# Input products of five FFN groups by a 2x2x2 Strassen scheme in an HGRN2 + maxout-FFN kernel

## The chip, the cores and the metric

The kernel runs on one core of one Trainium2 chip, in one launch. The metric is the device time in microseconds of that core. Times are given for the whole execution; the profile's span, which most views refer to, is a little shorter.

## What is computed

A recurrent attention block (4 batches, 8 heads, 768 steps, head size 48) feeds a feed-forward block with three input projections and a maximum over them, all in float32:

```python
for t in range(S):
    state = f[:, :, t, :, None] * state + np.einsum('bhd,bhe->bhde', k[:, :, t], v[:, :, t])
    y[:, :, t] = np.einsum('bhd,bhde->bhe', q[:, :, t], state)      # f = sigmoid(f_logit)
...
h = np.maximum(np.maximum(x @ w1, x @ w2), x @ w3)                  # x: (3072, 384), w: (384, 768)
return (h @ w_out).astype(np.float32)                               # w_out: (768, 384)
```

The weights come as 64-bit floats and are rounded to 32 bits in the kernel.

## The kernel before, in words

**Units and groups.** Attention is done in 24 units `u`, each 64 steps of two batches (128 tokens), in order. Four units make a group of TOK = 512 tokens; there are six groups, numbered 0 to 5 in the code and 1 to 6 in this text. The attended tokens of a group are kept transposed in `xT`, 128 partitions by NK = 3 blocks of 128 features by 512 tokens. When a group's attention is complete, its feed-forward part is queued as a generator in `pending`, and runs beside the attention of the next group.

**Attention of a unit.** ScalarE makes the gates (`sigmoids`, L296 or L299). VectorE scans the decays (L317, L335), transposes blocks of 32 (L284; L370 for `ks`, sixteen a unit), masks the score matrix (`at`, L383) and updates the state (L432). GpSimd multiplies the decays into keys and queries (`kh` L328, `qh` L339) and into the state (L345). TensorE forms scores (`pairs`, L380), values and state sums (`values`, L399 and L424) and the state's part (`finish`, L470). `finish` then copies the result to `heads` on ScalarE (L476), and `pack` (L484) moves it into `xT` by ten small DMAs on SP's queue: slots 0 to 2 of a group together, slot 3 alone, the latter at units 8, 12, 16, 20 and after unit 23. At the very end the ten are split between SP and ScalarE.

**Feed-forward of a group.** In groups 2 to 6 the maximum is taken relative to w1: `apart` (L545) has replaced w2 and w3 by their differences from w1, and `linear` (L561) has replaced w1 by w1 times w_out, so that the output is x times that (L528) plus the maximum of 0, x(w2-w1) and x(w3-w1), times w_out (L532). `ffn` (L605) makes, for each of six column blocks j, two products of three 128x128x512 matmuls (`product`, L511); ScalarE takes the first with Relu into `top` (L612), VectorE the maximum with the second into `hm` (L614). Then `outputs` (L524) makes four blocks of 128 tokens, each three matmuls L528 and six L532 of 384 columns, a ScalarE copy (L537) and two stores on SP. Products and outputs use the two PSUM buffers of pool `ps_f`; the two of `ps_tr` serve transposes, which units from 8 on no longer need. Group 1 (`ffn_first`, L572) does all three products, rounds the weights as they arrive, and does `apart`, the transposes of w1 (`turn`, L552) and `linear` behind its products.

**Order of the work.** The order on each engine is the order in which the code is written (`manual_schedule`). The main loop (L728) goes unit by unit, and between the steps of attention calls `fill`, which takes pieces of queued feed-forward work until their cost, 4/2.4 ns a column (COLUMN), has used up a budget. Each unit grants five times PART = 2740 ns (L643). An unused budget is kept while nothing is queued:

```python
def fill(ns):
    budget[0] += ns
    while budget[0] > 0 and pending:
        try:
            budget[0] -= next(pending[0])
        except StopIteration:
            pending.pop(0)
```

**Weights.** `load_weights` (L201) brings 24 pieces as 64-bit words into RAW = 12 staging buffers `raw`; `round_begin` and `round_end` turn them into float32 with `top_bits` (four buffers) and `rest_bits` (three). From unit 11 on `check_range` (L261) reads the pieces again on ScalarE and looks for values out of range, with the same buffers.

Of the kernel before, what the change touches and what calls it, by code (L numbers as in the profile page):

```python
# [9 lines left out]
FP32 = mybir.dt.float32  # L10
I32 = mybir.dt.int32
U32 = mybir.dt.uint32
AF = mybir.ActivationFunctionType
# [42 lines left out]
def kernel(  # L56
# [33 lines left out]
    def fast():  # L90
        ctx = ExitStack()
        with ctx:
# [100 lines left out]
            pieces = [(w_in[i][:, :, j * 128:(j + 1) * 128], src[:, j * 128:(j + 1) * 128])  # L193
                      for j in range(NJ) for i, src in enumerate((moe_w1, moe_w2, moe_w3))]
            pieces += [(w_out[:, j:j + 1, :], moe_w_out[j * 128:(j + 1) * 128, :]) for j in range(NJ)]
            RAW = 12
            PIECE = NK * 128
            raw, raw_next = {}, []

            def load_weights(count, done=0, queue=nc.sync):  # L200

                for n in range(len(raw_next), min(len(raw_next) + count, done + RAW, len(pieces))):
                    raw_next.append(n)
                    dst, src = pieces[n]
                    a = dst.shape[1]
                    if src.dtype != FP32:
                        raw[n] = work.tile([128, 2 * PIECE], U32, name="raw", bufs=RAW)
                        dst, src = raw[n].rearrange("p (a c) -> p a c", a=a), src.bitcast(U32)
                    queue.dma_start(out=dst, in_=src.rearrange("(a p) c -> p a c", a=a))

# [9 lines left out]

            BY_VECTOR = 9

            def round_begin(n):
                if n in raw:
                    lo, hi = words(n)
                    top = work.tile([128, PIECE], U32, name="top_bits", bufs=4)
                    if n >= BY_VECTOR:

                        nc.scalar.activation(top.bitcast(FP32), hi.bitcast(FP32), AF.Sign)
                        nc.scalar.mul(top.bitcast(FP32), top.bitcast(FP32), -2.0)  # L230

                    rest = work.tile([128, PIECE], U32, name="rest_bits", bufs=3)
                    nc.scalar.activation(rest, lo, AF.Copy, scale=2.0 ** -29)
                    halfway[n] = (top, rest)

# [17 lines left out]
            def check_load(n):  # L253
                src = pieces[n][1]
                if src.dtype != FP32:
                    raw[n] = work.tile([128, 2 * PIECE], U32, name="raw", bufs=RAW)
                    a = pieces[n][0].shape[1]
                    nc.sync.dma_start(out=raw[n].rearrange("p (a c) -> p a c", a=a),
                                      in_=src.bitcast(U32).rearrange("(a p) c -> p a c", a=a))

            def check_range(n):  # L261

                if n in raw:
                    _, hi = words(n)
                    size = work.tile([128, PIECE], FP32, name="top_bits", bufs=4)
                    over = work.tile([128, PIECE], FP32, name="rest_bits", bufs=3)
                    nc.scalar.activation(size, hi.bitcast(FP32), AF.Abs)
                    nc.scalar.activation(over, size, AF.Relu, scale=-1 / HI_MIN, bias=1.0,
                                         accum_out=outside[:, 2 * n:2 * n + 1])
                    nc.scalar.activation(over, size, AF.Relu, bias=-HI_END * (1 - 2.0 ** -24),  # L270
                                         accum_out=outside[:, 2 * n + 1:2 * n + 2])
                    raw.pop(n)
# [245 lines left out]
            def new_hm():  # L518
                return work.tile([128, NJ, TOK], FP32, name="hm", bufs=1)

            def new_top(w):
                return work.tile([128, TOK], FP32, name="top")[:, 0:w]
# [38 lines left out]
            def linear(a):  # L561

                p = ps_f.tile([128, TOK], FP32, name="p")
                for j in range(NJ):
                    nc.tensor.matmul(p[:, 0:DM], lhsT=w_in[0][:, a, j * 128:(j + 1) * 128], rhs=w_out[:, j, :],  # L565
                                     start=(j == 0), stop=(j == NJ - 1))
                    if j % 2:
                        if j == NJ - 1:
                            nc.scalar.copy(w_lin[:, a, :], p[:, 0:DM])
                        yield 2 * DM * COLUMN  # L570

            def ffn_first(xT):  # L572
                hm = new_hm()
# [22 lines left out]
                for i in range(GRP):  # L596
# [2 lines left out]
                    yield from outputs(0, hm, i)  # L599
                    for j in range(i * NJ // GRP, (i + 1) * NJ // GRP):  # L600
                        yield from turn(j)
                for a in range(NK):
                    yield from linear(a)

            def ffn(g, xT):  # L605
                hm = new_hm()
                for j in range(NJ):
                    for i in (1, 2):
                        p = yield from product(g, xT, j, i, slice(0, TOK))
                        if i == 1:  # L610
                            top = new_top(TOK)
                            nc.scalar.activation(top, p, AF.Relu)  # L612
                        else:
                            nc.vector.tensor_tensor(hm[:, j, :], p, top, op=ALU.max)  # L614
                        yield TOK * COLUMN
                for i in range(GRP):
                    yield from outputs(g, hm, i, xT)

# [425 lines left out]
```

## Time and profile before

| | |
|---|---|
| device time, median of 3 runs | 458.1 us (457.14 to 458.23) |
| the profiled execution | 457.98 us |
| its span | 456.2 us |
| granted TensorE clock | 1.00 |
| L511, 128x512, 432 records | 195.3 us busy |
| L532 and L528, 128x384, 408 records | 99.3 and 42.4 us busy |
| L370, 224 transposes of 32 rows | 67.7 us busy, 302 ns each |
| L614, 30 maxima of 512 columns | 681 ns each |
| L612, 30 Relu of 512 columns | 594 ns each |
| L328 and L339 on GpSimd, 512 columns | 1960 and 1176 ns each |
| `xT<-heads` DMAs | 588 ns between issues, 2.0 us from issue to landing (medians) |

The profile is of one execution. "Busy" is the time in which an engine has an instruction in work; "PE" are matmuls, "PEld" the loads of their stationary operand, DVE VectorE, ACT ScalarE, POOL GpSimd, SPq the queue of SyncE. A float32 matmul leaves two records. The columns of a group of instructions are: line, engine and operation, output<-inputs, shape and number, then busy time and the mean of one, then the engine's idle time ahead of them with what ended it. In a timeline the first number is the start from the begin of the span, the second the length, both in microseconds.

### The profile page before, as it was taken

The page shows a single profiled execution, that of the slowest core. Times are in us where ns is not written, and L with a number is a line of the kernel's source. Part 1 is how long each engine was busy: PE and PEld are TensorE (multiplying, and loading weights), DVE is VectorE, ACT ScalarE, POOL GpSimd, SP SyncE. Part 2 cuts the span into 40 slices and gives each one's busy share as a digit, 9 for nine tenths or more (in the row PEclk, how much of TensorE's full clock was granted, in tenths as well). Part 3 has the DMA queues.
Part 4 walks back from the last instruction along what each step waited for, and adds up shares of the span by engine and source line. Part 5 has one row for each costly group of instructions (what it writes and reads, how often), then busy time and mean ns, then how long its engine had stood idle before and what let it go on. Part 6 is the DMA issues. An engine that isn't in the chain of part 4 may idle for free.

```text
span 456.2 us, 10209 instructions
## 1 busy us (share of the span) xinstructions
PE 432.9 (95%) x4062; PEld 244.1 (54%) x4062; DVE 253.4 (56%) x510; ACT 150.1 (33%) x350; POOL 103.9 (23%) x125
## 2 busy tenths in 40 slices
PE   4989999999999999999999999999989999999995
PEld 3777655556554456554456654455544455544553
DVE  6976757556858569357779557759456520011100
ACT  2434757403312214414414524504324331111000
POOL 2153654403033033032033023023032120000000
PEclk9999999999999999999999999999999999999999
DMA  8889997202547733647763557643746003100011
GB/s 169 213 245 299 259 205 89 36 19 71 94 66 88 133 93 72 147 78 146 92 164 77 147 104 131 98 142 72 165 78 124 2 0 88 45 9 0 4 35 37
DMA packets 177140, 47.13 MB, mean 103 GB/s; under 512 B 154816, under 2 KB 175552, under 8 KB 177088
## 3 DMA queue, kind: packets, MB, share of 16 engines
q1 hardware_dynamic: 173616, 45.64, 47.6%
q10 hardware_dynamic: 3472, 0.79, 0.8%
q8 instruction: 33, 0.54, 0.5%
q14 instruction: 19, 0.16, 0.1%
HBM read 37.75 MB, written 4.72 MB: 93 GB/s over the span
## 4 chain that ended last, share of the span: by engine, by line
PE 84%; DVE 5%; ACT 4%; DMA 4%; issue 2%; SPq 1%; POOL 0%; ACTq 0%; DVEq 0%
PE p L511 42%; PE p L532 18%; PE p L528 7%; PE y L470 3%; PE p L565 3%; PE y L399 2%; PE y L424 2%; PE a L380 2%; DVE r L317 2%; DMA raw<-in_moe_w_out_dram 2%; ACT heads L476 1%; PE tr L279 1%; DMA xT<-heads 1%; ACT sig L299 1%; PE y L395 1%
## 5 line engine op out<-in xcount | busy, mean ns | idle before, releaser
L511 PE MATMUL p<-xT,w_in 128*128 128x512 f32 (+1 forms) x504 | 212.8, 569 | 7.5 <-ACT top L612 2.8
L511 PEld LDWEIGHTS p<-xT,w_in 128*128 128x128 f32 x504 | 92.0, 190 | 104.2 <-issue 85.2
L532 PE MATMUL p<-w_out,hm 128*128 128x384 f32 x288 | 99.3, 491 | 1.3 <-ACT w_in L558 1.0
L532 PEld LDWEIGHTS p<-w_out,hm 128*128 128x128 f32 x288 | 53.6, 190 | 37.1 <-ACT w_in L558 1.3
L370 DVE STREAM_TRANSPOSE ks<-kh 32x128 f32<-32x128 f32 x224 | 67.7, 302 | 3.5
L614 DVE TENSOR_TENSOR hm<-p,top 128x512 f32<-128x512 f32 x30 | 20.4, 681 | 80.9 <-PE p L511 80.5
L327 POOL COPY ends<-r 128x8 f32<-128x8 f32 x24 | 6.7, 279 | 187.0 <-DVE r L317 187.0
L612 ACT ACTIVATE top<-p 128x512 f32<-128x512 f32 x30 | 17.8, 594 | 91.9 <-PE p L511 91.9
L383 DVE TENSOR_TENSOR at<-a,mask 128x512 f32<-128x512 f32 x24 | 16.6, 692 | 48.8 <-PE a L380 48.8
L528 PE MATMUL p<-w_in,xT 128*128 128x384 f32 x120 | 42.4, 489 | 0.0
L537 ACT COPY o<-p 128x384 f32<-128x384 f32 x24 | 11.4, 477 | 93.6 <-PE p L532 90.1
L476 ACT COPY heads<-y 64x256 f32<-64x256 f32 (+1 forms) x60 | 22.1, 369 | 54.9 <-PE y L470 45.5
L328 POOL TENSOR_TENSOR kh<-kt,r 128x512 f32<-128x512 f32 x16 | 31.4, 1960 | 35.4 <-DVE kt L284 33.2
L317 DVE TENSOR_TENSOR_SCAN r<-gate,from_one 128x520 f32<-128x520 f32 x24 | 29.8, 1241 | 6.6 <-ACT gate L296 3.4
L528 PEld LDWEIGHTS p<-w_in,xT 128*128 128x128 f32 x120 | 22.5, 190 | 16.0 <-issue 1.9
L335 DVE TENSOR_TENSOR_SCAN prod<-gate,from_inv 128x520 f32<-128x520 f32 x24 | 30.2, 1257 | 0.0
L247 POOL TENSOR_TENSOR w_in<-top_bits,rest_bits 128x384 uint32<-128x384 uint32 x18 | 20.8, 1161 | 26.6 <-DVE top_bits L241 12.1
L339 POOL TENSOR_TENSOR qh<-qt,prod 128x512 f32<-128x512 f32 x16 | 18.8, 1176 | 6.2 <-DVE qt L284 6.2
L345 POOL TENSOR_TENSOR state<-st,ends 128x384 f32<-128x384 f32 x22 | 18.9, 857 | 0.2
L399 PEld LDWEIGHTS y<-at,v_ld 64*64 64x64 f32 x640 | 11.2, 134 | 13.0 <-issue 6.1
L380 PE MATMUL a<-qh,kh 48*64 48x64 f32 x768 | 15.7, 219 | 1.0 <-DVE qh L339 0.8
L470 PEld LDWEIGHTS y<-qh,state 48*48 48x48 f32 x640 | 10.3, 119 | 11.7 <-issue 11.7
(101 smaller groups left out, 366.3 us busy)
## 6 DMA issues: line engine op xcount, KB each, us to landing
raw<-in_moe_w_dram SPq DMA_DIRECT2D x36, 384.0 KB, 5.5
v_ld<-in_v_dram SPq DMA_DIRECT2D x48, 96.0 KB, 3.1
raw<-in_moe_w_out_dram SPq DMA_DIRECT2D x12, 384.0 KB, 4.9
out_dram<-o SPq DMA_DIRECT2D x47, 96.0 KB, 2.2
xT<-heads SPq DMA_DIRECT2D x30, 72.0 KB, 2.2
f_ld<-in_f_logit_dram SPq DMA_DIRECT2D x32, 64.0 KB, 2.7
k_ld<-in_k_dram SPq DMA_DIRECT2D x32, 64.0 KB, 2.7
q_ld<-in_q_dram SPq DMA_DIRECT2D x32, 64.0 KB, 2.9
```

The source lines that it names most:

```text
L247: nc.gpsimd.tensor_tensor(dst, by(top), by(rest), op=ALU.add)
L317: nc.vector.tensor_tensor_scan(r[:, 0:LEN][:, ::-1], flat(gate)[:, ::-1], flat(from_one)[:, ::-1], 1.0, op0=ALU.mult, op1=ALU.max)
L328: (nc.vector if u < BY_ROWS else nc.gpsimd).tensor_tensor(kh.rearrange("p h a t -> p a h t"), kt, by_batch(r[:, 1:LEN + 1].rearrange("p (x ...
L335: nc.vector.tensor_tensor_scan(flat(prod), flat(gate_tiles[u % 2]), flat(from_inv[u % 2]), 1.0, op0=ALU.mult, op1=ALU.max)
L370: nc.vector.transpose(ks[n * 32:(n + 1) * 32, :, par, e0:e0 + 32], kh[p0:p0 + 32, :, a, t0:t0 + 32])
L380: nc.tensor.matmul(p[t, par, hp * C:(hp + 1) * C], lhsT=kh[r, hp, a, :], rhs=qh[r, a, hp, :], start=True, stop=True)
L470: nc.tensor.matmul(y[o:o + D, a, hp * C:(hp + 1) * C], lhsT=st[r, a, hp, :], rhs=d["qh"][r, a, hp, :], start=False, stop=(hp == HP - 1), s ...
L476: nc.scalar.copy(heads[o, :, t0 + a * C:t0 + (a + 1) * C], y[i, a, 0:HP * C].rearrange("p (h t) -> p h t", h=HP))
L511: nc.tensor.matmul(p if g or w < TOK else p.rearrange("p (two t) -> p two t", two=2), lhsT=w_in[i][:, kt, j * 128:(j + 1) * 128], rhs=rhs, ...
L528: nc.tensor.matmul(p[:, 0:DM], lhsT=xT[:, kt, i * UT:(i + 1) * UT], rhs=w_lin[:, kt, :], start=(kt == 0), stop=False)
L532: nc.tensor.matmul(p[:, 0:DM], lhsT=hm[:, j, i * UT:(i + 1) * UT], rhs=w_out[:, j, :], start=(g == 0 and j == 0), stop=(j == NJ - 1))
L614: nc.vector.tensor_tensor(hm[:, j, :], p, top, op=ALU.max)
```

## The change

For groups 2 to 6 the input products are rearranged. The 512 tokens are split into two halves of 256, the two weight differences are taken together with two of the three feature blocks, and that 2x2x2 product is done with seven multiplications in place of eight; the third feature block is multiplied as before. Two column blocks share a PSUM bank. In this way a pair of column blocks takes 22 matmuls of 256 columns. Sums of tokens (`sx`, four of 128x256 a group) are made by VectorE; sums of weights (`mixed`) are made once, by five subtractions of 128x768 between the steps of `linear`, which is cut in halves. The results of the seven banks are joined by ScalarE (two copies, one Relu a pair), VectorE (five sums or maxima, one scalar_tensor_tensor) and GpSimd (two sums). Banks come in turn from `ps_f` and `ps_tr`. To make room, weights are staged in nine buffers, four of which (`raw_kept`) later hold the mixed weights, and the temporaries are shared with `top_bits` and `rest_bits`, now 512 columns wide. PART and the main loop stay.

```diff
-            RAW = 12
+            RAW, RAW_KEPT = 9, 4
+
+            def new_raw(kept=False):
+                return work.tile([128, 2 * PIECE], U32, name="raw_kept" if kept else "raw",
+                                 bufs=RAW_KEPT if kept else RAW - RAW_KEPT)
...
-                        raw[n] = work.tile([128, 2 * PIECE], U32, name="raw", bufs=RAW)
+                        raw[n] = new_raw(n % RAW >= RAW - RAW_KEPT)
...
+            def new_temp(name):
+                return work.tile([128, TOK], FP32, name=name, bufs=4 if name == "top_bits" else 3)
...
-                for a in range(NK):
-                    yield from linear(a)
+                for n in range(NJ):
+                    if n < 5:
+                        mix(n)
+                    yield from linear(n // 2, n % 2)
+
+            mixed = {}
+            first, second = w_in[1], w_in[2]
+
+            def mix(n):
+
+                if n == 0:
+                    mixed.update({i: new_raw(True).bitcast(FP32) for i in (2, 3, 4, 5)})
+                    mixed[1] = second[:, 0]
+                out, x, y = ((mixed[3], second[:, 1], second[:, 0]), (mixed[1], second[:, 0], first[:, 0]),
+                             (mixed[2], second[:, 1], mixed[1]), (mixed[4], first[:, 1], mixed[2]),
+                             (mixed[5], first[:, 2], second[:, 2]))[n]
+                nc.vector.tensor_tensor(out, x, y, op=ALU.subtract)
 
             def ffn(g, xT):
+
                 hm = new_hm()
-                for j in range(NJ):
-                    for i in (1, 2):
-                        p = yield from product(g, xT, j, i, slice(0, TOK))
-                        if i == 1:
-                            top = new_top(TOK)
-                            nc.scalar.activation(top, p, AF.Relu)
-                        else:
-                            nc.vector.tensor_tensor(hm[:, j, :], p, top, op=ALU.max)
-                        yield TOK * COLUMN
+                X = lambda k, half: xT[:, k, half * HALF:(half + 1) * HALF]
+                sx = work.tile([128, 4, HALF], FP32, name="sx", bufs=1)
+                S = lambda n: sx[:, n - 1]
+                two = lambda t: t.rearrange("p (j t) -> p j t", j=2)
+                turn_of = [0]
+
+                def bank(j, *terms):
+                    turn_of[0] += 1
+                    p = ps_f.tile([128, TOK], FP32, name="p") if turn_of[0] % 2 else ps_tr.tile([128, TOK], FP32, name="tr")
+                    for jj in range(2):
+                        for n, (w, x) in enumerate(terms):
+                            nc.tensor.matmul(p[:, jj * HALF:(jj + 1) * HALF], lhsT=w[:, (j + jj) * 128:(j + jj + 1) * 128],
+                                             rhs=x, start=(n == 0), stop=(n == len(terms) - 1))
+                    return p, 2 * len(terms) * HALF * COLUMN
+
+                def add(out, x, y, op=ALU.add, engine=nc.vector):
+                    engine.tensor_tensor(out, x, y, op=op)
+
+                for j in range(0, NJ, 2):
+                    out = [hm[:, j:j + 2, h * HALF:(h + 1) * HALF] for h in range(2)]
+                    p, cost = bank(j, (first[:, 0], X(0, 0)))
+                    e1 = new_temp("top_bits")
+                    nc.scalar.copy(e1, p)
+                    yield cost
+                    p, cost = bank(j, (first[:, 1], X(1, 0)), (first[:, 2], X(2, 0)))
+                    a = new_top(TOK)
+                    add(a, p, e1)
+                    yield cost
+                    if j == 0:
+                        add(S(3), X(0, 0), X(0, 1), ALU.subtract)
+                        add(S(1), X(0, 1), X(1, 1))
+                        add(S(2), S(1), X(0, 0), ALU.subtract)
+                        add(S(4), X(1, 0), S(2), ALU.subtract)
+                    p4, cost = bank(j, (mixed[4], X(1, 1)), (mixed[5], X(2, 1)))
+                    yield cost
+                    p, cost = bank(j, (mixed[1], S(1)))
+                    e5 = new_temp("top_bits")
+                    nc.scalar.copy(e5, p)
+                    d = new_temp("rest_bits")
+                    add(d, p4, e5, ALU.max)
+                    yield cost
+                    p, cost = bank(j, (mixed[2], S(2)))
+                    m = new_temp("top_bits")
+                    add(m, p, e1)
+                    add(d, d, m, engine=nc.gpsimd)
+                    yield cost
+                    p, cost = bank(j, (second[:, 1], S(4)), (second[:, 2], X(2, 0)))
+                    q = new_temp("rest_bits")
+                    add(q, p, e5)
+                    add(q, q, m, engine=nc.gpsimd)
+                    yield cost
+                    p, cost = bank(j, (mixed[3], S(3)), (second[:, 2], X(2, 1)))
+                    add(out[1], two(p), two(d))
+                    nc.scalar.activation(out[1], out[1], AF.Relu)
+                    nc.vector.scalar_tensor_tensor(out[0], two(a), 0.0, two(q), op0=ALU.max, op1=ALU.max)
+                    yield cost
                 for i in range(GRP):
                     yield from outputs(g, hm, i, xT)
```

The seven banks of a pair are called bank 1 to bank 7 in this text, in the order of the code. In the changed kernel the products stand at L644, `at` at L390, `ks` at L377, L424 at L431, L470 at L477, L528 at L535, L532 at L539, and the DMAs of `pack` at L498.

More of the change, by code (lines that the diff above doesn't have):

```diff
@@ L225, in round_begin @@
                     lo, hi = words(n)
-                    top = work.tile([128, PIECE], U32, name="top_bits", bufs=4)
+                    top = new_temp("top_bits")[:, 0:PIECE].bitcast(U32)
                     if n >= BY_VECTOR:
@@ L230, in round_begin @@
                         nc.scalar.mul(top.bitcast(FP32), top.bitcast(FP32), -2.0)
-                    rest = work.tile([128, PIECE], U32, name="rest_bits", bufs=3)
+                    rest = new_temp("rest_bits")[:, 0:PIECE].bitcast(U32)
                     nc.scalar.activation(rest, lo, AF.Copy, scale=2.0 ** -29)
@@ L255, in check_load @@
                 if src.dtype != FP32:
-                    raw[n] = work.tile([128, 2 * PIECE], U32, name="raw", bufs=RAW)
+                    raw[n] = new_raw()
                     a = pieces[n][0].shape[1]
@@ L264, in check_range @@
                     _, hi = words(n)
-                    size = work.tile([128, PIECE], FP32, name="top_bits", bufs=4)
-                    over = work.tile([128, PIECE], FP32, name="rest_bits", bufs=3)
+                    size = new_temp("top_bits")[:, 0:PIECE]
+                    over = new_temp("rest_bits")[:, 0:PIECE]
                     nc.scalar.activation(size, hi.bitcast(FP32), AF.Abs)
@@ L559, in turn, with linear @@
                 yield DM * COLUMN
-            def linear(a):
-                p = ps_f.tile([128, TOK], FP32, name="p")
-                for j in range(NJ):
-                    nc.tensor.matmul(p[:, 0:DM], lhsT=w_in[0][:, a, j * 128:(j + 1) * 128], rhs=w_out[:, j, :],
+            lin = {}
+            def linear(a, half):
+                if half == 0:
+                    lin[a] = ps_f.tile([128, TOK], FP32, name="p")
+                p = lin[a][:, 0:DM]
+                for j in range(half * NJ // 2, (half + 1) * NJ // 2):
+                    nc.tensor.matmul(p, lhsT=w_in[0][:, a, j * 128:(j + 1) * 128], rhs=w_out[:, j, :],
                                      start=(j == 0), stop=(j == NJ - 1))
[L567 to L570, printed above, removed]
+                if half:
+                    nc.scalar.copy(w_lin[:, a, :], p)
+                yield NJ // 2 * DM * COLUMN
             def ffn_first(xT):
@@ L605, in ffn @@
             def ffn(g, xT):
                 hm = new_hm()
-                for j in range(NJ):
-                    for i in (1, 2):
-                        p = yield from product(g, xT, j, i, slice(0, TOK))
-                        if i == 1:
-                            top = new_top(TOK)
-                            nc.scalar.activation(top, p, AF.Relu)
-                        else:
-                            nc.vector.tensor_tensor(hm[:, j, :], p, top, op=ALU.max)
-                        yield TOK * COLUMN
+                X = lambda k, half: xT[:, k, half * HALF:(half + 1) * HALF]
```

## Prediction

> **What bounds the kernel now.** I read the page's busy shares first, then the groups by shape, the stretches from one group of tokens to the next, and the timeline at the seams between groups.
>
> ```profile
> PE 432.9 (95%) x4062; PEld 244.1 (54%) x4062; DVE 253.4 (56%) x510; ACT 150.1 (33%) x350; POOL 103.9 (23%) x125
> ...
> L511 PE MATMUL p<-xT,w_in 128*128 128x512 f32 x432 | 195.3, 600 | 6.6 <-ACT top L612 2.8 <-DVE hm L614 1.9 <-DMA xT<-heads 1.8
> L614 DVE TENSOR_TENSOR hm<-p,top 128x512 f32<-128x512 f32 x30 | 20.4, 681 | 80.9 <-PE p L511 80.5
> ```
>
> TensorE is busy nearly always; VectorE waits for it (80.5 us before L614), hardly ever the reverse (1.9 us). So work taken from TensorE shortens the span, as long as nothing else is late. Now the stretches between the ends of L470 at group seams (each line: the stretch, its length, then the busy time of PE, PEld, DVE, ACT and POOL):
>
> ```profile
> 119.60:187.80 68.20, 66.84 (x644) 35.63 (x635) 46.22 (x103) 16.18 (x37) 16.31 (x16) 1.00 0.52 94
> 187.80:254.90 67.10, 65.55 (x685) 35.20 (x688) 46.01 (x102) 25.64 (x66) 16.36 (x16) 1.00 0.59 118
> 254.90:323.80 68.90, 67.33 (x680) 35.88 (x672) 46.07 (x102) 25.87 (x67) 16.33 (x16) 1.00 0.57 114
> 323.80:390.70 66.90, 64.34 (x608) 33.58 (x599) 27.30 (x50) 22.10 (x58) 12.27 (x12) 1.00 0.33 70
> 390.70:451.40 60.70, 60.59 (x174) 30.75 (x166) 4.97 (x11) 6.66 (x15) 0.00 (x0) 1.00 0.09 21
> ```
>
> TensorE fills every stretch, the last (no attention left) without a gap, but in three of them VectorE already has 46 us of 67 to do. Last, the timeline (start, length): a run of 256-column products, the seam at 323 and the seam at 390.
>
> ```profile
> 42.65 2.76 PE L511 MATMUL p<-xT,w_in 128*128 128x256 f32 x12
> 45.24 0.60 PE L279 MATMUL tr<-ident,q_ld 128*128 128x128 f32 x4
> ...
> 323.36 0.66 PE L470 MATMUL y<-qh,state 48*48 48x64 f32 x32
> 326.77 6.79 SPq L491 DMA_DIRECT2D xT<-heads  x10
> 331.50 1.12 PE L511 MATMUL p<-xT,w_in 128*128 128x512 f32 x2
> 334.47 1.96 PE L511 MATMUL p<-xT,w_in 128*128 128x512 f32 x4 [1.84 <-DMA xT<-heads]
> ...
> 390.73 2.20 PE L528 MATMUL p<-w_in,xT 128*128 128x384 f32 x6
> 391.95 3.59 SPq L491 DMA_DIRECT2D xT<-heads  x5
> 392.77 4.03 PE L532 MATMUL p<-w_out,hm 128*128 128x384 f32 x12
> 396.64 23.34 PE L511 MATMUL p<-xT,w_in 128*128 128x512 f32 x54
> 419.91 0.19 PE L792 MATMUL tr<-is_feature,least 128*1 128x1 f32 x2
> ```
>
> A matmul is two records. The reader is to see that at a seam the last quarter of xT travels by ten DMAs, which land some 10 us after L470 (6 us at the last seam, where two queues share the issues), and that outputs of the group before (L528, L532) fill just that time.
>
> [...] here a float32 load takes 190 ns (L511 PEld)[...] four transposes take 0.86 us from 6.85 to 7.71, and 0.44 us from 18.00 to 18.44. [...] L383 has 692. [...] L339 takes 1176 ns and the same size at L328 1960 ns[...].
>
> **The change, part by part.** The sum is made against the profiled execution, 457.98 us (span 456.2), beside a median of 458.1.
>
> *Matmuls.* A group had 36 products of 512 columns (6 column blocks, 2 weights, 3 feature blocks); now 3 pairs of blocks with 11 terms, 2 blocks each, are 66 products of 256 columns. 512 columns: from 396.64 to 419.91 are 27 matmuls, 0.862 us each, up to 0.87 in the run behind it; I take 0.864. 256 columns: 42.65 to 45.24 are 6 in 2.59 us, 0.432 each. Five groups: 180 x 0.864 = 155.5 us become 330 x 0.432 = 142.6: **-12.9 us**. Two weight loads (2 x 0.19 = 0.38) still fit under 0.432, but barely; bounds -8 (0.447 a product) and -14.
>
> *Seams.* fill() counts columns. A group costs its budget 51.2 us (28.2 + 23.0) instead of 53.8, while PART, five times for each of four units, still grants 54.8. So outputs are used up earlier, and in the order of the changed program less of them stands behind the last L470 of a group. Bank 3 of the new scheme is the first to read the second half of xT; in front of it stand banks 1 and 2, 6 x 0.432 = 2.6 us, and one product of its own.
> Seam at unit 12: L380 0.6, three blocks of three outputs 5.8, L399 and L424 1.2 and banks 2.6 make 10.2 us against a landing after 9.5: nothing. At 8: over 14 us: nothing.
> At 16: 0.6 + 1.9 + 1.2 + 3.0 = 6.7 us, landing after 9.3 (first issue 256.14, last 262.4, 1.9 to land; L470 ends at 255.0): +2.5.
> At 20: L380 and the banks alone, 3.6 us, landing after 10.4 (334.4 less 324.0), or 9 if SP is free at once: about +6.2, where now 1.8 are lost: +4.4.
> Last seam: 3.0 us against 5.9 (390.7 to 396.6): +2.9, since the 5.9 us of L528 and L532 that covered it are now done before.
> Behind the waiting bank 3 stands all of TensorE's later work. The half-width sums wait for the same DMAs on VectorE; behind them stand kt, the scan prod and qt, and GpSimd waits for these, but it is TensorE that ends last there.
> Sum **+9.8**, bounds 3 and 13.
>
> *VectorE.* Removed for each group: 6 maxima, 4.1 us. Added: 15 of 512 columns with PSUM, 0.65 from start to start, 3 scalar_tensor_tensor of two SBUF inputs (no row; 0.65 to 1.1 from L550, 650 ns for 384; I take 0.7) and 4 sums of half width (0.42, from L585): 13.5 us. A unit of attention costs it 16 x 0.302 (L370) + 3 x 0.70 (L284) + 1.24 + 1.26 + 0.21 + 0.69 + 0.53 = 10.9. In the product stage, some two units long, that is 21.8 + 13.5 = 35.3 us, against 28.5 + 2 x 2.3 = 33.1 of TensorE. VectorE works in order: what is late behind its new operations is the mask of `at`, the transposes of ks (L424 waits) and the release of banks. Following the order through group 3 (unit 12) by hand: bank 4 waits 1.1 for the half-width sums, L424 0.7 for ks, the first output 1.1 for hm, whose last step waits for GpSimd (kh 1.96, qh 1.18, state 0.83, then two new additions of 1.2 to 2.0): 2.9 us, where 1.5 are lost now (0.7 + 0.6 + 0.2). Group 2 comes to 2.1 for 1.3. Four groups: 0.8 + 1.4 + 1.4 + 0.8, the last with half the ks work: about **+4**, bounds 0 and 11. Four banks instead of two is why it isn't more. In group 6 VectorE is free, nothing is added.
>
> *ScalarE*: nine operations of 0.59 for six, +1.8 us a group, under 26 of 67 busy: nothing. Its new Relu waits for VectorE's sum into hm, and behind it queue the copy of the next pair's first bank and the heads copies; four banks bear that wait. *GpSimd*: 30 additions, 6 a group; only the wait above.
>
> *Start*: five subtractions of 768 columns (1.0 to 1.3 us each from L550), spread between VectorE's work while 18 products L565 run; nine instead of twelve staged weight pieces still lead their use by six roundings. **+0.5**, bounds 0 and 3: SP would hold loads queued behind a piece whose buffer GpSimd has not freed.
>
> *Clock*: of the 6 us at unit 20 about 4.5 lie in one piece[...]. Half a chance: **+1**, bounds 0 and 3.5.
>
> Sum: -12.9 + 9.8 + 4 + 0.5 + 1 = +2.4, so **460.4 us**.
>
> **Rivals.** (1) *The seams stay covered, not slower.* Place: bank 3 at units 16, 20 and the end; price: up to 9.8 us; it decides below about 6 us in all. For it: SP may issue earlier where the outputs' stores are already gone, and a TensorE delayed by VectorE gives the DMAs time. Against it: heads copies, ten issues of 0.65 and 1.9 to land are fixed. With 3.5 us at the seams, 3 at VectorE and 0.5 at the start: -5.9, 452 us. (2) *VectorE becomes the bound.* For it: 35 of 33 us[...]; against it: four banks, and output stages in which it can catch up. +10 instead of +4: 466.5. (3) *The narrow products don't keep 0.432 us*, since loads leave 0.05 of it: at 0.447, 465.
>
> **How the numbers follow.** Forecast 0.45 (own range 457 to 463.5), rival 1 0.28, rival 2 0.18, rival 3 0.09. The range 451.5 to 467 leaves out the lower end of rival 1 and the upper of 2. A measurement of this kernel tells about 0.3%, 1.4 us, from no change: below 456.6 lies most of rival 1, 0.27; between, its rest and the lower part of the forecast, 0.18; above 459.4, 0.55.
>
> **What would show it.** (Lines of the changed kernel here: L644 the products, L431 today's L424.) L644 x660 records near 0.216 us from start to start; PE's waits of L644 for DMA xT<-heads of 2 to 7 us near units 16, 20 and the end; VectorE busy near 300 us, 56 of 66 in a group's stretch; L644 and L431 (ks) waiting for DVE, 2 to 3 us a group. Wrong if the seams show no gap of TensorE over 2 us, or if its gaps inside the product stages sum to over 15 us.

## The result, and the profile after

| | before | changed |
|---|---|---|
| device time, median | 457.6 us (456.18 to 458.23, 4 runs) | 474.9 us (473.24 to 475.2, 4 runs) |
| the profiled execution | 457.98 us | 474.79 us |
| its span | 456.2 us | 473.1 us |
| mean granted TensorE clock | 1.00 | 0.977 |

The ratio is 1.0375 (95% interval 1.0339 to 1.0411): 17 us slower. The forecast was 460.4 us with a range up to 467; the sign was right, the size was not.

First the page of the changed kernel: busy times, and the clock that was granted in 40 slices of the span.

```profile
PE 433.1 (92%) x4362; PEld 308.8 (65%) x4362; DVE 306.9 (65%) x595; ACT 157.7 (33%) x365; POOL 144.0 (30%) x155
...
PEclk9989999999999999999999989989979999999999
```

TensorE was busy for 432.9 us before and is for 433.1 now, although its products need 12.9 us less. "Busy" counts a matmul at half clock at nearly twice its length (six records of L644 take 2.90 us in place of 1.53, below), so the saving must have been eaten inside the busy time as well as in gaps. The clock row says where: slices below 9 near 30, 278, 313 and 349 us (a slice is 11.8 us long; the half clock from 294.46 to 297.88 us lies across a border, and hides in two 9s). In the profile of before no slice lies below 9. Next, what TensorE waited for (in total, times, longest):

```profile
PE p L644 <- DMA xT<-heads: 13.9, 7, 6.7
PE tr L644 <- DVE rest_bits L649: 4.7, 2, 2.4
PE y L431 <- DVE ks L377: 3.7, 8, 1.3
PE p L644 <- DVE rest_bits L649: 2.0, 1, 2.0
```

For xT it was 1.8 us before. The stretches between the starts of L477 at the seams (stretch, length, busy time of PE, PEld, DVE, ACT and POOL, clock, DMA share, GB/s), to be set beside those of before in the prediction:

```profile
121.24:191.08 69.84, 66.80 (x730) 48.69 (x729) 61.52 (x126) 17.75 (x40) 25.64 (x22) 1.00 0.48 86
191.08:262.98 71.90, 67.44 (x729) 48.38 (x729) 55.58 (x118) 27.78 (x70) 23.83 (x22) 1.00 0.58 115
262.98:340.33 77.35, 70.32 (x724) 51.07 (x723) 56.00 (x118) 27.14 (x69) 23.90 (x22) 0.93 0.51 103
340.33:412.38 72.05, 64.06 (x654) 46.73 (x653) 36.64 (x66) 23.44 (x60) 20.40 (x18) 0.95 0.31 67
412.38:473.00 60.62, 53.41 (x241) 39.09 (x240) 14.13 (x27) 8.68 (x17) 7.60 (x6) 0.99 0.09 21
```

The second to fourth were 67 to 69 us and are now 72, 77 and 72; VectorE has gone from 46 to 56 us in two of them. The clock stands below 1 in the two that grew most. Last, the seam that the prediction showed at 323 us, now at 340:

```profile
340.33 0.66 PE L477 MATMUL y<-qh,state 48*48 48x64 f32 x32
...
342.36 1.89 PE L644 MATMUL tr<-xT,w_in 128*128 128x256 f32 x8
...
350.91 1.19 PE L644 MATMUL p<-xT,raw_kept 128*128 128x256 f32 x2 [6.66 <-DMA xT<-heads]
352.83 2.90 PE L644 MATMUL p<-xT,raw_kept 128*128 128x256 f32 x6 [0.73 <-DMA xT<-heads]
355.52 1.22 PE L644 MATMUL tr<-sx,w_in 128*128 128x256 f32 x4
356.57 1.03 PE L644 MATMUL p<-sx,raw_kept 128*128 128x256 f32 x4
```

Two banks cover 2.6 us, then nothing is ready for 6.7 us. And then look at the lengths: six records of bank 3 take 2.90 us where six take 1.53 at the last seam (at 419.01, with the clock at 1.00). It is the same instruction; the clock that was granted from 349.07 to 355.90 us is 0.50.

**The sum.** Taking TensorE's records from start to start, the 16.8 us between the two profiled executions split as follows: products -12.9; gaps and waits at the seams +12.1 (13.9 less 1.84); VectorE's lateness +7.4 (4.7 us more of gaps on L649, L377 and the like, and 2.7 inside the records of L431, 13.28 to 15.97); half clock +8.9, an estimate: half of the 17.8 us in which TensorE was busy at a granted clock of 0.50 (six windows of 3.41 us, so up to 1.7 us for each); the rest, shared among transposes and the start, +1.3.

### The profile page after: what moved, and what is told of

It is laid out like the page before. It is cut to its first block, busy times and chain, and to the rows that moved or that the text cites. A ratio compares the mean times of both kernels' runs of the same rounds, so it can differ in the third digit from the quotient of the medians.

```text
span 473.1 us, 11016 instructions
## 1 busy us (share of the span) xinstructions
PE 433.1 (92%) x4362; PEld 308.8 (65%) x4362; DVE 306.9 (65%) x595; ACT 157.7 (33%) x365; POOL 144.0 (30%) x155
## 4 chain that ended last, share of the span: by engine, by line
PE 63%; DVE 12%; SPq 8%; DMA 8%; ACT 3%; issue 3%; POOL 1%; ACTq 1%; DVEq 0%; POOLq 0%
PE p L539 18%; PE p L518 10%; PE p L644 9%; PE tr L644 8%; PE p L535 7%; SPq L183 4%; SPq L498 3%; DVE ks L377 3%; DMA xT<-heads 2%; DMA f_ld<-in_f_logit_dram 2%; DVE rest_bits L649 2%; DVE r L324 2%; PE y L477 1%; PE y L431 1%; PE y L406 1%
## 5 line engine op out<-in xcount | busy, mean ns | idle before, releaser
L539 PE MATMUL p<-w_out,hm 128*128 128x384 f32 x288 | 100.8, 498 | 1.2 <-ACT w_in L565 1.0
L539 PEld LDWEIGHTS p<-w_out,hm 128*128 128x128 f32 x288 | 54.4, 193 | 38.5 <-issue 2.2
L377 DVE STREAM_TRANSPOSE ks<-kh 32x128 f32<-32x128 f32 x224 | 67.7, 302 | 3.5
L649 POOL TENSOR_TENSOR rest_bits<-rest_bits,top_bits 128x512 f32<-128x512 f32 x30 | 37.7, 1269 | 97.4 <-DVE top_bits L649 91.2
L518 PE MATMUL p<-xT,w_in 128*128 128x256 f32 (+1 forms) x144 | 51.4, 503 | 1.0 <-DVE hm L595 0.7
L334 POOL COPY ends<-r 128x8 f32<-128x8 f32 x24 | 7.7, 321 | 123.0 <-DVE r L324 123.0
L390 DVE TENSOR_TENSOR at<-a,mask 128x512 f32<-128x512 f32 x24 | 16.6, 691 | 43.7 <-PE a L387 43.5
L535 PE MATMUL p<-w_in,xT 128*128 128x384 f32 x120 | 42.6, 491 | 0.5 <-DVE top_bits L649 0.5
L644 PE MATMUL tr<-xT,w_in 128*128 128x256 f32 x160 | 42.9, 386 | 0.0
L644 PE MATMUL p<-xT,w_in 128*128 128x256 f32 x140 | 37.9, 381 | 0.0
L518 PEld LDWEIGHTS p<-xT,w_in 128*128 128x128 f32 x144 | 26.9, 196 | 16.6 <-issue 12.7
L644 PE MATMUL p<-xT,raw_kept 128*128 128x256 f32 x80 | 22.9, 426 | 13.9 <-DMA xT<-heads 13.9
L686 ACT ACTIVATE hm<-hm 128x512 f32<-128x512 f32 x15 | 9.5, 630 | 77.2 <-DVE hm L649 77.2
L644 PEld LDWEIGHTS tr<-xT,w_in 128*128 128x128 f32 x160 | 30.8, 194 | 4.4
L535 PEld LDWEIGHTS p<-w_in,xT 128*128 128x128 f32 x120 | 22.3, 190 | 14.8 <-DVE top_bits L649 0.9
L483 ACT COPY heads<-y 64x256 f32<-64x256 f32 (+1 forms) x60 | 22.1, 368 | 26.5 <-PE y L477 25.3
L644 PEld LDWEIGHTS p<-xT,w_in 128*128 128x128 f32 x140 | 26.5, 191 | 4.1
```

The source lines that it names most:

```text
L377: nc.vector.transpose(ks[n * 32:(n + 1) * 32, :, par, e0:e0 + 32], kh[p0:p0 + 32, :, a, t0:t0 + 32])
L483: nc.scalar.copy(heads[o, :, t0 + a * C:t0 + (a + 1) * C], y[i, a, 0:HP * C].rearrange("p (h t) -> p h t", h=HP))
L518: nc.tensor.matmul(p if g or w < TOK else p.rearrange("p (two t) -> p two t", two=2), lhsT=w_in[i][:, kt, j * 128:(j + 1) * 128], rhs=rhs, ...
L535: nc.tensor.matmul(p[:, 0:DM], lhsT=xT[:, kt, i * UT:(i + 1) * UT], rhs=w_lin[:, kt, :], start=(kt == 0), stop=False)
L539: nc.tensor.matmul(p[:, 0:DM], lhsT=hm[:, j, i * UT:(i + 1) * UT], rhs=w_out[:, j, :], start=(g == 0 and j == 0), stop=(j == NJ - 1))
L644: nc.tensor.matmul(p[:, jj * HALF:(jj + 1) * HALF], lhsT=w[:, (j + jj) * 128:(j + jj + 1) * 128], rhs=x, start=(n == 0), stop=(n == len(te ...
```

## The experiments

**Pace alone: PART fitted to the cheaper group.**

```diff
-            PART = 2740
+            PART = 2640
```

> The changed kernel with PART = 2640 instead of 2740, so that each of the five grants of a unit is smaller by as much as the new group is cheaper (51.2 instead of 53.8 us); arithmetic and instructions are the same, only the interleaving moves. By the order of the program 17.2, 15.2, 12.1, 12.1 and 8.4 us of TensorE work then stand between L477 and bank 3 at the five seams (14.1, 10.2, 6.3, 3.2 and 2.6 in the changed kernel), against landings after 9.3 to 10.4 us (6 at the last). Theory (outputs used up too early, the exposed wait and the half-rate clock behind it): PE's waits of L644 for xT<-heads fall from 13.9 us to under 2, the half-rate windows at 274 and 349 to 356 us go, -12 and -4: 457 to 460 us. Rival (VectorE is the bound, the seams are only where TensorE waits for it anyway): the waits move to L644 <- DVE, 468 us or more.

459.75 us, ratio 1.0038 (1.0017 to 1.0058). 15 us of the loss are gone by a number in the pacing; the instructions are the same, only their order differs. The waits of TensorE now:

```profile
PE y L431 <- DVE ks L377: 6.1, 12, 1.5
PE tr L644 <- DVE sx L649: 5.5, 2, 2.8
...
PE p L644 <- DVE rest_bits L649: 2.0, 1, 2.0
PE tr L644 <- ACT top_bits L655: 1.6, 1, 1.6
```

No wait for xT is left, and the half-rate windows at the seams are gone (two others remain, at 139 and 207 us, behind waits for VectorE of 2.7 and 2.8 us; the mean clock of this execution is 0.992). So the exposed seams were a cost of their own, not slack in front of another bound. But the rival was half right as well: the products' 12.9 us don't come out, since TensorE now waits some 15 us for VectorE and, in one place, for a copy on ScalarE (the four lines above).

**The clock alone: TensorE kept busy in the waits.** In front of bank 3 stand 5 (unit 16) and 14 (unit 20) added products into its own tile, which its first real product overwrites:

```diff
+                    for _ in range(warm):
+                        nc.tensor.matmul(p[:, 0:HALF], lhsT=first[:, 0, 0:128], rhs=X(0, 0), start=True, stop=True)
...
-                    p4, cost = bank(j, (mixed[4], X(1, 1)), (mixed[5], X(2, 1)))
+                    p4, cost = bank(j, (mixed[4], X(1, 1)), (mixed[5], X(2, 1)), warm={3: 5, 4: 14}.get(g, 0) if j == 0 else 0)
```

> The changed kernel with 5 (unit 16) and 14 (unit 20) extra products of 256 columns ahead of bank 3, written into bank 3's own tile before its first product overwrites them: 2.2 and 6.0 us of work in gaps of 2.8 and 7.4 us. The waits for the DMAs stay, but TensorE isn't idle in them. If the clock is a cost of its own: no half-rate window at 274 and 349 to 356 us, and 4 us less than the changed kernel, about 471. If the half rate costs nothing beside the waits: 475, unchanged.

470.21 us: 4.7 less than the changed kernel, with 19 useless products more. The seam at unit 20 with it (L643 are the added products, L646 the old L644):

```profile
336.68 6.21 PE L643 MATMUL p<-xT,w_in 128*128 128x256 f32 x28
343.60 0.67 PE L646 MATMUL p<-xT,raw_kept 128*128 128x256 f32 x2 [0.71 <-DMA xT<-heads]
345.51 1.53 PE L646 MATMUL p<-xT,raw_kept 128*128 128x256 f32 x6 [1.25 <-DMA xT<-heads]
346.88 1.03 PE L646 MATMUL tr<-sx,w_in 128*128 128x256 f32 x4
```

xT lands as late as ever (10.7 and 12.6 us after the start of L477 at 332.93; 10.6 and 12.5 in the changed kernel), but the six records that follow take 1.53 us instead of 2.90. The profiled execution had no half-rate window at all and took 466.03 us, 8.8 below the changed kernel's 474.79, where the half clock had been counted at 8.9. Not all of this is the edit's: it fills the waits at two seams, and the three windows behind these (274 and 349 us) were counted at 3.8 us, near the 4.7 of the medians. That the windows at 31.6, 294.5 and 314.9 us were missing too is luck of this execution. The others (469 to 471 us) had a mean clock of 0.987 to 0.995 against 0.999 in this one.

**The joins alone.** All joins of the new scheme, VectorE's and GpSimd's, on 64 of 512 columns (`few` takes 32 of each half). The rest of the maximum is left out; ScalarE writes the Relu of two raw banks in its place:

```diff
-                    engine.tensor_tensor(out, x, y, op=op)
+                    engine.tensor_tensor(few(out), few(x), few(y), op=op)
...
-                    nc.scalar.activation(out[1], out[1], AF.Relu)
+                    nc.scalar.activation(out[1], two(p), AF.Relu)
+                    nc.scalar.activation(out[0], two(e5), AF.Relu)
...
```

> The changed kernel with the joins of the new scheme (VectorE's and GpSimd's) on 64 of 512 columns; the rest of the maximum is left out, and ScalarE writes Relu of two raw banks in its place, so the output is not the maximum. Matmuls, order and seams stay. Theory (VectorE's lateness costs about 7 us, and two half-rate windows at 294 and 315 us some 3.4 more; the seams cost the rest): L644 <- DVE and L431 <- ks waits vanish, the seam waits stay near 14 us, 464 to 467 us. Rival (VectorE is the bound): 458 or less. If VectorE costs nothing of its own: 473 to 475.

463.76 us, 11.1 less than the changed kernel. The wait for xT stays (13.4 us in all), L431's wait for ks falls from 3.7 to 0.6. So there are two costs: pacing takes 15.1 us and thin joins 11.1. They are not independent: with pacing alone the waits for VectorE grow (ks from 3.7 to 6.1, `sx` from 0.2 to 5.5 us), and the two together, below, take 22.1 and not 26.2. The run thins GpSimd's sums along with VectorE's, so it does not tell the two engines apart.

**The old products with the same exposure.** The kernel before with PART = 2880, which grants 57.6 us for a group of 53.8, 7% too much, as the changed kernel's 54.8 for 51.2:

```diff
-            PART = 2740
+            PART = 2880
```

> The kernel before, with PART = 2880 instead of 2740: same arithmetic, old products, but each unit is granted more than a group costs, so that outputs are used up early, as in the changed kernel (57.6 us granted for 53.8). Theory: exposure of the seams costs the same without the new scheme: waits of the products for xT<-heads of 12 to 20 us and half-rate windows behind them, 470 to 480 us. Rival (it is the new scheme's VectorE work that makes the seams late): near 458 to 462.

484.2 us, ratio 1.0573 (1.0521 to 1.0625), more than expected: the waits for xT sum to 22.7 us, and 31 us of the span lie in half-rate windows (mean clock 0.966), some 9.1 us of lost time by the same estimate as above. At unit 20 (start, length, what was waited for):

```profile
339.62 0.66 PE L470 MATMUL y<-qh,state 48*48 48x64 f32 x32
340.10 0.65 PE L380 MATMUL a<-qh,kh 48*64 48x64 f32 x32
350.34 2.05 PE L511 MATMUL p<-xT,w_in 128*128 128x512 f32 x2 [9.59 <-DMA xT<-heads]
```

No Strassen scheme is needed for the loss at the seams. A budget 7% above what a group costs is enough.

**Pace and thin joins together.**

> Both at once: PART = 2640 and the new scheme's joins on 64 of 512 columns (the rest of the maximum is left out, as in the run with thin joins alone). Theory (exposed seams and VectorE's lateness, with the half-rate windows behind each, are all that stands against the products' -12.9 us): 457.5 - 12.9 = 444.6, so 444 to 448 us, no wait of PE over 1.5 us after 60 us. Rival (a third cost, such as the narrow products themselves): 452 us or more.

452.75 us: above what was expected, on the rival's side. It isn't the products (256 columns take 0.432 us in it as in all others). TensorE still waits 4.8 us for the half-width sums `sx`, which thin joins leave as they are, 2.7 for joins, and lost 1.7 to a half-rate window behind a wait of 1.6 for a copy on ScalarE (L656; mean clock 0.995). Thin joins were late here too, where they stood in line behind something. What VectorE's queue looks like at such a place is best seen in the changed kernel itself, in the stage of group 4 (timeline; only VectorE's lines and the waiting one of TensorE):

```profile
287.32 0.69 DVE L390 TENSOR_TENSOR at<-a,mask 128x512 f32<-128x512 f32 x1
287.93 0.70 DVE L291 STREAM_TRANSPOSE gate<-sig 128x512 f32<-128x512 f32 x1
288.67 1.24 DVE L324 TENSOR_TENSOR_SCAN r<-gate,from_one 128x520 f32<-128x520 f32 x1
...
290.18 1.28 DVE L377 STREAM_TRANSPOSE ks<-kh 32x128 f32<-32x128 f32 x4
...
291.49 0.71 DVE L291 STREAM_TRANSPOSE kt<-k_ld 128x512 f32<-128x512 f32 x1
292.13 1.20 DVE L342 TENSOR_TENSOR_SCAN prod<-gate,from_inv 128x520 f32<-128x520 f32 x1
...
293.25 0.68 DVE L291 STREAM_TRANSPOSE qt<-q_ld 128x512 f32<-128x512 f32 x1
293.85 0.65 DVE L649 TENSOR_TENSOR rest_bits<-tr,top_bits 128x512 f32<-128x512 f32 x1
...
294.56 1.22 PE L644 MATMUL tr<-sx,raw_kept 128*128 128x256 f32 x2 [2.38 <-DVE rest_bits L649]
```

From 287.32 to 293.85, 6.5 us, VectorE has only attention's steps. TensorE wants the bank back at 292.18, and gets it when the join behind all that is done, at 294.5. The join's own 0.65 us are the smallest part. Not every such wait is work in line alone. In the stage of group 3 TensorE waits as long for the same kind of join. There VectorE itself had stood idle for 2.9 us until a load landed that `qt` needed, while the joins behind `qt` were ready:

```profile
220.79 0.71 DVE L291 STREAM_TRANSPOSE qt<-q_ld 128x512 f32<-128x512 f32 x1 [2.90 <-DMA f_ld<-in_f_logit_dram]
...
223.20 0.70 PE L644 MATMUL tr<-sx,raw_kept 128*128 128x256 f32 x2 [2.36 <-DVE rest_bits L649]
```

In both the join stands behind attention's steps. This made a new theory: it is the order on VectorE that costs. VectorE took its instructions in the order of the program (in the first of the two timelines `at`, gate, r, ks, kt, prod, qt and the join, from 287.32 to 294.50 us), and this order is set by five large grants a unit, with whole blocks of attention's steps between them.

**The order alone.** Seven grants of 1886 in place of five of 2640, so that joins come between smaller pieces; no instruction added or removed:

```diff
-            PART = 2740
+            PART = 2640 * 5 // 7
...
+                    fill(PART)
                     if n < NU:
                         sigmoids(n)
                         scan(n)
...
                     if n < NU:
                         after(n)
+                    fill(PART)
+                    if n < NU:
                         before(n)
                     fill(PART)
```

> The changed kernel with seven grants of 1886 in place of five of 2640 a unit (13.2 us of columns a unit in both): one more grant ahead of sigmoids and scan, one between after and before, so that VectorE's attention steps (at 0.7, gate and scan 2.1, kt 0.7, prod and qt 1.9 us) no longer stand in one piece ahead of joins. Same instructions. If the lateness comes from joins that stand in line behind such pieces: PE's waits for VectorE fall from some 15 us to under 8, no half-rate window, 448 to 454 us. If it is VectorE's whole load (some 56 of 66 us): 457 to 460 us, as with five grants.

451.62 us, ratio 0.985 (0.9817 to 0.9882), 8.1 below five grants, a little more than the thin joins won (7.0, 452.75). Order is thus a cost of its own. But the waits fell less than expected, from some 15 us to 10.8, not under 8. The largest:

```profile
PE y L431 <- DVE ks L377: 4.1, 7, 1.7
PE tr L644 <- DVE sx L649: 2.7, 2, 2.2
PE tr L644 <- DVE rest_bits L649: 2.1, 2, 1.9
```

Then with thin joins on top:

> Seven grants of 1886 and the joins of the new scheme on 64 of 512 columns (the rest of the maximum is left out). With five grants of 2640 and thin joins, 452.75 us, TensorE still waited 4.8 us for the half-width sums and lost 1.7 to a half-rate window: sums that stood in line behind attention's VectorE steps. If VectorE's order and load are all that is left against the products: 444 to 448 us. If something else takes a share (450 us or more), it is neither order nor load of VectorE.

441.71 us, below what was expected, and 9.9 below the full joins in the same order. Order isn't all then: the load of the joins counts too. The time lies below even 444.6 us, the kernel before less the products' 12.9. That fits the control below, in which the kernel before gains from the spreading as well. Spreading without the pacing:

> The changed kernel with seven grants of 1957, which is five of 2740: spread, but paced as before, with 3.2 and 2.6 us of TensorE work ahead of bank 3 at unit 20 and the end. If the seams and VectorE's order are two costs that add (459.75 with pacing alone, 451.62 with both, 474.9 with neither): the seam waits stay near 13 us with their half-rate windows, 463 to 468 us. If spreading alone cures it: below 458 us.

466.77 us, as expected. Pace and order add up:

| | five grants | seven grants |
|---|---|---|
| PART as it was (13.7 us a unit) | 474.89 | 466.77 |
| fitted (13.2 us a unit) | 459.75 | 451.62 |

That is 15.1 us by the pace in both columns, 8.1 by the order in both rows; that the two agree to the last digit is luck, since executions of one of these kernels differ by 2 to 5 us.

**The control: the same spreading in the kernel before.**

> The kernel before with the same spreading alone: seven grants of 1957 for five of 2740. Control: the old scheme has two joins in a column block and waits some 3 us on them in all, so 455 to 459 us, no difference that can be told. If spreading helps any kernel of this shape: 454 us or less, and then the gain with it in the changed kernel isn't the new scheme's.

451.94 us, ratio 0.9858 (0.9818 to 0.9897): a miss, and an important one. The kernel before gains 5.6 us from it too (457.51 to 451.94); of its waits, those on hm (1.9 us) and xT (1.8 us) are gone. So 451.62 is no merit of the new scheme: at equal spreading the two are level. TensorE's gaps sum to 16.8 us in the changed kernel against 8.5 in the one before, and L431's records take 15.3 us against 12.7: 11 us of waiting for 11 us of products (207.6 less 196.7). With one grant more, between the last ks block and kt, for the changed kernel and then for the one before:

> The changed kernel with eight grants of 1650 (one more between the last ks block and kt): the joins stand behind at most 2.9 us of attention's steps, ks is the last piece taken apart. If what is left of the waits (ks 4.1, sums 2.7, joins 3.3 us with seven grants) is still order: 449 to 451 us. If it is load by now: 451 to 453 us, unchanged.

> The kernel before with eight grants of 1712 (the same 13.7 us of columns a unit): the control for the changed kernel with eight grants (449.44). With seven it took 451.94; its waits for VectorE are down to some 2 us there, so there is little left: 450.5 to 452.5 us. Then the new scheme is worth 1 to 3 us at equal spreading. If it falls to 449.5 or less, the new scheme is worth nothing at equal spreading, and all that was won came from the order.

449.44 us (ratio to the kernel before 0.981, 0.9752 to 0.9869) for the changed kernel, 451.65 (0.9868, 0.9846 to 0.9889) for the one before: with this grant the new scheme is some 2 us ahead by the medians, but the two intervals overlap. The changed kernel's largest wait that is left after the start, with its queue on VectorE (timeline of the changed kernel with eight grants):

```profile
138.05 0.69 DVE L390 TENSOR_TENSOR at<-a,mask 128x512 f32<-128x512 f32 x1
138.66 0.68 DVE L649 TENSOR_TENSOR top<-tr,top_bits 128x512 f32<-128x512 f32 x1
139.25 0.70 DVE L291 STREAM_TRANSPOSE gate<-sig 128x512 f32<-128x512 f32 x1
139.99 1.24 DVE L324 TENSOR_TENSOR_SCAN r<-gate,from_one 128x520 f32<-128x520 f32 x1
...
141.47 0.76 DVE L649 TENSOR_TENSOR sx<-xT 128x256 f32<-128x256 f32 x2
142.27 0.42 DVE L649 TENSOR_TENSOR sx<-sx,xT 128x256 f32<-128x256 f32 x1
...
142.29 1.13 PE L644 MATMUL tr<-sx,w_in 128*128 128x256 f32 x4 [2.96 <-DVE sx L649]
```

The half-width sums are what bank 4 reads, and stand behind at, a join, gate and scan. They need nothing but xT, which has landed: bank 3, which reads its second half too, ran from 137.44.

**The sums ahead.** Eight grants, and the four sums issued before a group's first bank:

```diff
                 for j in range(0, NJ, 2):
                     out = [hm[:, j:j + 2, h * HALF:(h + 1) * HALF] for h in range(2)]
+                    if j == 0:
+                        add(S(3), X(0, 0), X(0, 1), ALU.subtract)
+                        add(S(1), X(0, 1), X(1, 1))
+                        add(S(2), S(1), X(0, 0), ALU.subtract)
+                        add(S(4), X(1, 0), S(2), ALU.subtract)
...
-                    if j == 0:
...
```

> The changed kernel with eight grants of 1650, and the four half-width sums issued ahead of a group's first bank instead of behind its second: 4 to 5 us earlier in VectorE's order, while the previous group's outputs still cover the landing. With eight grants TensorE waited 4.6 us for them. If they were late because they stood in line behind at, gate, scan and ks: that wait goes, 444 to 446.5 us. If VectorE is full there and only hands the wait on to the next join: 448 to 450 us. If they now wait for xT's DMAs and hold the attention steps behind them: 451 us or more.

445.1 us, ratio 0.9729 (0.9703 to 0.9755): faster than the kernel before by 2.7%, and than the kernel before in the same order by 6.5 us. The waits for `sx` are gone from the list, but part of them was handed on to joins:

```profile
PE p L644 <- DVE rest_bits L649: 3.4, 3, 2.0
PE tr L644 <- DVE rest_bits L649: 2.5, 3, 1.3
```

These two were 1.5 and 0.8 us with eight grants. In all, TensorE's gaps fell by 2.2 us (15.0 to 12.9) between the two profiled executions. Another 1.7 of the 3.5 us between them is a half-rate window at 31.9 us, which the one with eight grants alone had (mean clock 0.996) and this one had not (0.999); it lies before the new scheme begins, so the sums have no part in it. VectorE is now close to full:

```profile
118.00:186.00 68.00, 64.46 (x724) 46.87 (x723) 63.75 (x130) 19.17 (x44) 25.55 (x22) 1.00 0.54 100
186.00:252.00 66.00, 64.85 (x724) 47.76 (x723) 56.62 (x119) 27.50 (x71) 23.68 (x22) 1.00 0.59 114
```

In the stretch in which the new scheme begins, VectorE (third of the engines) is busy for 63.75 of 68 us, and for 57 of 66 in the next.

**Where VectorE has room.** The new scheme in the last group only, with five grants of 2740, then in the last two (from group 5 on, with grants of 2640 from unit 20). `ffn_old` is the old `ffn`; the five weight subtractions stand among the outputs of the last group that it does:

```diff
...
-                            pending.append(ffn(u // GRP - 1, xT))
+                            pending.append((ffn if u // GRP - 1 >= 5 else ffn_old)(u // GRP - 1, xT))
...
```

> The new scheme in group 6 alone, where no attention runs beside it; groups 2 to 5 keep the old products, PART stays 2740, the five weight subtractions stand among the outputs of group 5. Theory (the scheme pays where VectorE is free and the seam is covered): 12 x 3 products of 0.864 become 66 of 0.432, -2.6 us, 454.5 to 455.5 us. Rival (it costs by itself): 457 us or more.

> The new scheme in groups 5 and 6, subtractions among the outputs of group 4, PART = 2740 before unit 20 and 2640 from there. Theory: -5.2 us of products, some 1 us back for VectorE in group 5's stage, where half of the ks transposes still run: 453 to 455 us. Rival (VectorE's lateness costs as much as the products give wherever attention runs beside them): 455 to 457 us, as with group 6 alone or worse.

455.75 us (ratio 0.9947, 0.9929 to 0.9964) and 454.5 us (0.9927, 0.9901 to 0.9953). That is a gain of about 2.5 us for the first (458.23 to 455.75), as its products give, and another 1.2 for the second, which the intervals do not tell apart. With eight grants, sums ahead:

> Old products in groups 2 to 4, the new scheme in groups 5 and 6, eight grants (1712, from unit 20 on 1650), sums ahead. -5.2 us of products against the kernel before with eight grants, where VectorE has room: 446 to 448 us. If order is all that VectorE's lateness is, the new scheme in all five groups (sums ahead) is 4 us or more below this one; if its load costs as well where attention runs in full, this one is level or ahead.

447.18 us. Against the kernel before in the same order (451.65) the last two groups bring 4.5 of 5.2 us; the three others bring 2.1 more (447.18 to 445.1) of their 7.7. So where VectorE has room, nearly the whole saving comes out, and where attention runs in full beside it, a quarter. The expectation's two cases were 4 us or more if order is all, and none if load costs as well; the measured 2.1 lie between. The missing three quarters fit VectorE's load, since the order is the same. It is not shown that they are VectorE's alone: no run thins its joins and leaves GpSimd's sums as they are.

## Why the prediction was wrong, step by step

**Matmuls, -12.9: right.** In the changed kernel 56 products of 256 columns take from 420.38 to 444.56, 0.432 us each, weight loads and all; start to start, without the half-clock share, all products (group 1 included) went from 208.8 to 195.9 us. Rival 3 falls.

**Seams, +9.8: right in kind, 12.1 measured.** Waits of 1.2, 2.8, 7.4 and 2.5 us at units 12, 16, 20 and the end, forecast 0, 2.5, 6.2 and 2.9. What was too small is the landing: at units 12 and 20 the ten issues begin 4.2 us after the start of L477 (195.26 less 191.08, 344.55 less 340.33), behind output stores and two loads on SP, where they began 1.5 and 3.4 us after the start of L470 before. Counted from the end of L477, as in the forecast, the last feature block lets TensorE go on after 11.9 us at unit 12 and 11.8 at unit 20, not 9.5 and 10.4. Pace alone removes all of the waits; the old products with a wrong pace have them too. Rival 1 falls.

**VectorE, +4: right in kind, 7.4 measured, one wait overlooked.** The forecast followed one group by hand and found bank 4, ks and hm late, and said that four banks keep it from being more. It named the release of banks among what would be late, but put no time to it. The largest single waits are just those, for a bank whose join stands behind attention's steps: 2.0, 2.4 and 2.4 us. Four banks hold some 5.4 us of products (4 x 22/7 x 0.432), and a piece of attention's work on VectorE is up to 6.5 us long. Rival 2 put +10 here; the 7.4 lie between it and the forecast.

**Start, +0.5: right**, apart from a half-rate window at 31.6 us: to the first seam the changed kernel takes 2.1 us more (121.24 less 119.10), of which 1.7 are this window. The kernel before with seven grants has such a window as well (at 31.9 us; mean clock 0.996).

**Clock, +1: the step that failed.** It priced one window with half a chance, and only at unit 20, for a gap of about 4.5 us in one piece. That it takes so long a gap was an estimate that nothing had shown: the profile of before has slow records only behind its first wait of 5.12 us (four transposes take 0.86 us from 6.85), and from 8.8 us on its clock is 1.00 until TensorE's work is done. In the changed kernel five stretches ran at half clock, six windows of 3.41 us, and cost 8.9 us by the estimate above, 7.2 of them behind waits that the change made. Only one of the five, at 349 us, follows so long a gap (6.66 us). The three behind the other waits of the change follow gaps of 2.20 us (to 272.12), of 2.38 us (to 294.56), and of 1.26 and 0.34 us (to 312.83 and 313.49). The second is the wait shown above, after which two records take 1.22 us, where the first two after a wait took 0.67 with TensorE kept warm. Keeping TensorE busy through the waits at two seams, with xT landing as late as before, gave 4.7 us back in the median, where the windows behind these two had been counted at 3.8. So the cost of half clock behind these waits is shown at these seams; the 8.9 for all windows is an estimate from the profile, which no run shows by itself.

The terms that were off are thus 7.9 (clock), 3.4 (VectorE) and 2.3 us (seams), with 0.8 of rest: the 14.4 us between 460.4 and 474.8. The clock term alone moves the sum to 468.3.

## What to carry to other kernels

When work that fills the gaps of a schedule is made cheaper, the budget that paces it has to be cut as much, or the filler is used up before the places that it covered; and the pieces of work that share an engine and are taken in the order of the program, as on VectorE here, have to be laid between each other. Here this was worth 8.1 us to the changed kernel and 5.6 to the one before. Price a wait of TensorE above its length: in the changed kernel the wait of 2.38 us that ends at 294.56 was followed by 3.41 us at half clock, with TensorE busy for 3.31 of them, which is another 1.7 us by the estimate above. Compare a change with the old code spread in the same way: 451.62 looked like a gain of 6 us for the new scheme until the control took 451.94.

## What was not expected of the hardware

In the changed kernel's trace the granted clock falls to 0.50 in windows of 3.413 us, and these lie on a grid: they begin at 31.6, 274.0, 294.5, 314.9 and 349.1 us (two), distances that are whole multiples of 3.413 (71, 77, 83 and 93 from the first; one more begins at 472.0, when TensorE's work is done). Take the time without a matmul record in each window of this grid (the start of the kernel, to 12 us, and its end left out). Of the windows at full clock, those with 2.16, 2.29 and 3.41 us idle were followed by one at half clock, and none with 1.42 us or less was; between them both happened (1.47 and 1.60 yes, 1.50, 1.51 and 1.94 no). How a wait lies on the grid may thus count beside its length: the wait of 2.38 us that ends at 294.56 fell within one window (2.29 us of it), and the next ran at half clock; the one of 2.36 us that ends at 223.20, ahead of the same instruction, lay on both sides of a border (1.94 and 0.42 us) and slowed nothing, its two records taking 0.70 us and not 1.22. With TensorE kept warm at the seams, a wait for the same kind of join was 2.4 us long as well, and the mean clock of that execution was 0.999. What decides between 1.42 and 2.16 us stays open. This may also be why executions of a kernel with such waits differ, though only the profiled ones have their windows on record: pace alone took 456.9 to 462.2 us in 20 runs, those with a mean clock of 0.984 from 460.8 to 462.2, those with 0.991 or more from 456.9 to 458.6.
